# Unused identity products on TensorE while the first chunk's attention is computed

## Chip, core, metric

The kernel runs on one core of a Trainium2 chip. The metric is the device time of one execution in microseconds (us), median of several executions. Engines are named as the profile names them: PE is TensorE (PEld its weight loads), DVE is VectorE, ACT is ScalarE, POOL is GpSimd, SP is SyncE, whose queue here issues every DMA.

## What is computed

An attention block feeds two feed-forward blocks, all in float32. Cut to what matters:

```python
# q, k, v: (4, 8, 576, 64)
q_d, k_d, v_d = means of q, k, v over groups of 4 positions
out_up   = repeat(softmax(q_d k_d^T / 8) v_d, 4)
out_loc  = softmax(where(|i - j| < 4, q k^T / 8, -1e9)) v
x        = (out_up + out_loc) as (2304, 512)
h        = x @ w_in                      # 512 x 2048
x        = (h - tanh(h)) @ w_out         # 2048 x 512
gate     = sigmoid(x @ w_gate)           # 512 x 1536
out      = (gate * (x @ w_val)) @ w_out2 # 1536 x 512
```

## The kernel before

The 2304 tokens are cut into six chunks of 384. For each chunk the first feed-forward block runs over sixteen slices f of its hidden width: `do_h` makes a slice of h, `h_out` and `g_out` turn it into h - tanh(h), `do_y` multiplies that back and adds into four PSUM banks `acc0` to `acc3`. Each float32 product of these blocks is taken as three products of split operands (`mm3`, lines 227 to 229; the split is lines 221 to 223 and line 237).

Attention is emitted as a list of items. A "down" item (`down`) is the pooled attention of one pair of heads: scores (line 300), the maximum (line 315), exponentials (line 321), normalising (lines 282 to 288), two transposes by the identity `id_sb` (line 329) and the values (line 341). A "local" item (`local`) is the banded attention of six blocks of 64 queries: scores (line 367), scale and mask (lines 404 or 411), maximum (line 415), exponentials (line 419), normalising, transposes (line 427), values (line 435) and the addition of the two attentions (line 450). The pooled means of q and k are line 268 on DVE for the first batch, lines 270 to 272 on POOL for the others.

Nothing of the first feed-forward block can start before the attention of the first chunk, so the program begins with a loop (lines 626 to 634) that emits one attention item after the other and, between them, parts of the first two slices of h (`early_h`, banks `acc2` and `acc3`), loads of weights (`w_load`) and the conversion of weights from float64 bits to float32 (lines 168, 174, 176, 191). `tick` advances a counter by which later steps of an item are emitted. A second loop (lines 635 to 637) emits what is left of `early_h`. From line 638 on the first chunk's slices follow one another, with later attention items between them.

PSUM has eight banks here: `acc0` to `acc3` and four of tag `ab`. Every step of attention takes its bank from `a_bank`. While `startup[0]` is true, two of each six go to `acc0` and `acc1`, which `do_y` doesn't need yet; the other four go round the four `ab` banks.

The order on PE, DVE and ACT in this opening part is not the order of the code: a scheduler places the instructions of these engines from their dependences and its own costs. POOL's order is as written, SP's from the first chunk on, ACT's, DVE's and POOL's from the second chunk on.

Of the kernel before, what the change touches and what calls it, by code (L numbers as in the profile page):

```python
# [52 lines left out]
def tile_kernel(ctx: ExitStack, tc: tile.TileContext, qk, vp, v, w1, w2, mask, ident, out):  # L53
    nc = tc.nc
# [22 lines left out]
    id_sb = const.tile([128, 128], F32, name="id_sb")  # L77
# [3 lines left out]
    startup, spare = [True], [0]  # L81

    def acc_bank(e):
        return ps.tile([128, 512], F32, tag=f"acc{e}", name="acc")

    def a_bank():

        spare[0] += 1
        if startup[0] and spare[0] % 6 in (2, 4):
            return acc_bank(spare[0] % 6 // 2 - 1)  # L90
        return ps.tile([128, 512], F32, tag="ab", bufs=4, name="ab")


# [13 lines left out]
    def run_chains(todo):  # L107
        while todo:
            for g in list(todo):
                if next(g, True):  # L110
                    todo.remove(g)

    def tick():
        now[0] += 1
        run_chains(chains.pop(now[0], []))
        todo = events.get(now[0], [])
        while todo:
            fn, args = todo.pop(0)
            fn(*args)
        events.pop(now[0], None)  # L120
        if beat[0]:
            beat[0]()
# [6 lines left out]
    def raw_pool(i):  # L129
        if i < n_a:  # L130
            return rawp if i % (n_b + 1) == n_b else raw1
        if i < U1:
            return rawp
        return rawp if (i - U1) % 2 else wpools["raw2"]
# [12 lines left out]
    def w_load(limit):  # L147

        while loaded[0] < min(limit, n_units if "raw2" in wpools else U1):
            i = loaded[0]  # L150
            raws[i] = raw_pool(i).tile([128, WU], I64, tag="raw", name="raw")
            nc.sync.dma_start(out=raws[i], in_=w1[i] if i < U1 else w2[i - U1])
            load_at[i] = now[0]
            loaded[0] += 1
# [5 lines left out]
    def w_begin(limit=n_units):  # L160
        i = begun[0]
        if i >= min(limit, loaded[0]) or now[0] < load_at[i] + 5:
            return
        begun[0] += 1
        hi = words(i)[1].bitcast(F32)


        nc.scalar.activation(out=hi, in_=hi, func=ACTF.Prelu, scale=2.0 ** -112, alpha=2.0 ** 32)
        chain(2, w_bits, i)
        defer(5, w_high, i)  # L170
# [38 lines left out]
    def weight(l, f, j):  # L209

        i, at = (f, 512 * j) if l == 1 else divmod((3 * f + j) * 512, WU)
        i += U1 * (l - 1)
        while i not in wt:
            tick()
        return wt[i][:, :, at:at + 512]

    def have(l, f, j):
        return f in wt
# [74 lines left out]
    def down(u):  # L293
        m = means.pop(u)
        qd, kd = m[:, 0, :], m[:, 1, :]
        sd = a_bank()[:, :3 * SD].rearrange("p (j k) -> p j k", j=3)
        for j in range(3):
            for h in range(2):
# [27 lines left out]
        def turn(f):  # L326
            tb = a_bank()[:72, :384]
            for j in range(3):
                nc.tensor.transpose(  # L329
                    out=tb[:, 128 * j:128 * j + 128], in_=pd[:, j, 72 * f:72 * f + 72], identity=id_sb  # L330
                )

            kept = bass.AP(tensor=tb.tensor, offset=tb.offset, ap=[list(tb.ap[0]), [64, 2], [136, 3], [1, 48]])
            defer(1, copy, pdt[:, f], kept)

        def values():
            vd = vds.pop(u)
            ob = a_bank()[:, :SD]
            for h in range(2):
                for f in range(2):  # L340
                    nc.tensor.matmul(
                        out=ob[64 * h:64 * h + 64, :], lhsT=vd[:, f, 64 * h:64 * h + 64],
                        rhs=pdt[:, f, h].rearrange("p j k -> p (j k)"), start=(f == 0), stop=(f == 1),
                    )
            defer(1, copy, od[:, p % 2, :], ob)
# [153 lines left out]
    def item():  # L499

        fetch()
        x = items[started[0]]
        if x[0] == "d" and x[1] not in means:
            return 0
        started[0] += 1
        if x[0] == "d":
            down(x[1])
            return 4
        local(*x[1:])
        return 6  # L510
# [15 lines left out]
    def h_part(w, key, bank, k):  # L526
        wh, wl = (w[:, i, k * 128:(k + 1) * 128] for i in range(2))
        x = xt[key, k]
        mm3(bank[:, :N], wh, wl, x[:, 0, :], x[:, 1, :], k == 0, k == KD - 1)
# [11 lines left out]
    def h_out(c, f, hb):  # L541
        h_done.add((c, f))
        t = ts[c, f] = xs.tile([128, N], F32, tag="xs", name="t")
        nc.scalar.activation(out=t, in_=hb[:, :N], func=ACTF.Tanh)  # L544
        chain(1, subtract, t, hb[:, :N], t)
        defer(2, g_out, c, f)
# [66 lines left out]
    def early_h(n):  # L613
        for _ in range(n):
            if not early:
                return
            k, f = early[0]
            if ((1, 0), k) not in xt or not have(1, f, 0) or now[0] < seen.setdefault((k, f), now[0] + 3):
                return
            early.pop(0)  # L620
            h_part(weight(1, f, 0), (1, 0), hbs[f], k)
            if k == KD - 1:
                h_out(0, f, hbs[f])

    free = [0]
    while any(((1, 0), k) not in xt for k in range(KD)):
        if now[0] >= free[0] and started[0] < len(items):
            item()
        early_h(2)
        tick()  # L630
        w_load(min(loaded[0] + 1, 3))
        if started[0] % 3 == 0:
            w_begin(U1)
        tick()
    while early:
        early_h(1)
        tick()
    startup[0] = False

# [162 lines left out]
```

## Time and profile before

| | us |
|---|---|
| median of 3 runs (lowest, highest) | 1038.02 (1035.78, 1040.18) |
| the profiled execution | 1036.53 |
| its span, first to last instruction | 1034.7 |
| PE busy in the span | 992.7 (96%) |
| DVE busy | 422.3 (41%) |
| ACT busy | 373.1 (36%) |

The profiled execution's own time is 1.8 us longer than its span and 1.5 us shorter than the median. [...] Averages over the span hide the opening part, which is 85 us of 1035; it has to be read in windows.

### The profile page before, as it was taken

The numbers are of one execution on the slowest core, as the hardware profiler recorded it, in microseconds if no ns is written. First come the engines' busy times: TensorE is split into PE (matmuls) and PEld (weight loads), VectorE is DVE, ScalarE is ACT, GpSimd is POOL, SyncE is SP. The second block draws the span as 40 slices with busy tenths as digits, with TensorE's granted clock in tenths as the row PEclk, the third lists the DMA queues.
The fourth block names the chain that finished last, engine by engine and source line by source line (L and its number), as shares of the span: only waits on it lengthen the run. The fifth ranks groups of instructions, "written<-read, shape, count | busy, mean of one in ns | idle before, by whom it ended". The sixth has DMA issues, their size and how long they took to land.

```text
span 1034.7 us, 15463 instructions
## 1 busy us (share of the span) xinstructions
PE 992.7 (96%) x6392; PEld 923.6 (89%) x6392; DVE 422.3 (41%) x736; ACT 373.1 (36%) x951; POOL 81.5 (8%) x89
## 2 busy tenths in 40 slices
PE   3889999999999999999999999999999999999997
PEld 2658988999999899999999899999999999999996
DVE  5788774324334444433765654113211113211112
ACT  5666554334334344433643543113111113111111
POOL 2251220110110302000000000000000000000000
PEclk9568999999999999999999999999999999999998
DMA  9543732301301411203535231001100002000001
GB/s 295 182 167 114 259 87 78 93 24 56 107 3 55 125 28 47 78 17 120 167 111 185 89 123 41 1 23 39 61 1 1 1 24 69 32 1 1 1 1 62
DMA packets 33111, 76.74 MB, mean 74 GB/s; under 512 B 3264, under 2 KB 23184, under 8 KB 28688
## 3 DMA queue, kind: packets, MB, share of 16 engines
q1 hardware_dynamic: 33040, 75.75, 22.6%
q8 instruction: 50, 0.82, 0.3%
q14 instruction: 21, 0.17, 0.1%
HBM read 63.15 MB, written 12.58 MB: 73 GB/s over the span
## 4 chain that ended last, share of the span: by engine, by line
PE 88%; DVE 5%; ACT 3%; DMA 3%; issue 1%; POOL 0%; SPq 0%; DVEq 0%; ACTq 0%; POOLq 0%
PE ab L227 18%; PE ab L228 17%; PE ab L229 17%; PE acc L227 9%; PE acc L228 9%; PE acc L229 9%; PE ab L367 2%; PE ab L435 2%; PE ab L427 1%; PE ab L300 1%; DMA raw<-in_w 1%; DVE raw L176 1%; DMA qk<-in_qk 1%; DVE w L191 1%; PE ab L329 1%
## 5 line engine op out<-in xcount | busy, mean ns | idle before, releaser
L227 PE MATMUL ab<-x,w 128*128 128x384 f32 x952 | 326.7, 343 | 3.7 <-ACT x L237 3.7
L228 PE MATMUL ab<-x,w 128*128 128x384 f32 x952 | 322.4, 339 | 0.0
L229 PE MATMUL ab<-x,w 128*128 128x384 f32 x952 | 321.7, 338 | 0.0
L227 PEld LDWEIGHTS ab<-x,w 128*128 128x128 f32 x952 | 179.1, 188 | 10.6 <-ACT x L237 4.4
L228 PEld LDWEIGHTS ab<-x,w 128*128 128x128 f32 x952 | 179.4, 188 | 3.5 <-DVE x L222 0.3
L229 PEld LDWEIGHTS ab<-x,w 128*128 128x128 f32 x952 | 179.4, 188 | 0.0
L728 DVE TENSOR_TENSOR p<-ab,p 128x384 f32<-128x384 f32 x72 | 40.1, 557 | 277.6 <-PE ab L229 277.6
L227 PE MATMUL acc<-g,w 128*128 128x384 f32 x384 | 133.9, 349 | 0.0
L228 PE MATMUL acc<-g,w 128*128 128x384 f32 x384 | 129.9, 338 | 0.0
L229 PE MATMUL acc<-g,w 128*128 128x384 f32 x384 | 129.7, 338 | 0.0
L240 DVE TENSOR_TENSOR t<-ab,t 128x384 f32<-128x384 f32 x94 | 52.3, 556 | 156.8 <-ACT t L544 156.7
L724 ACT ACTIVATE p<-ab 128x384 f32<-128x384 f32 x72 | 35.3, 491 | 187.2 <-PE ab L229 187.2
L544 ACT ACTIVATE t<-ab 128x384 f32<-128x384 f32 x94 | 45.8, 487 | 153.3 <-PE ab L229 137.4
L237 ACT ACTIVATE g<-p 128x384 fp32r<-128x384 f32 x72 | 37.8, 525 | 157.5 <-DVE p L728 157.5
L227 PEld LDWEIGHTS acc<-g,w 128*128 128x128 f32 x384 | 72.1, 188 | 2.5 <-issue 2.0
L228 PEld LDWEIGHTS acc<-g,w 128*128 128x128 f32 x384 | 72.2, 188 | 0.1
L229 PEld LDWEIGHTS acc<-g,w 128*128 128x128 f32 x384 | 72.1, 188 | 0.0
L240 DVE TENSOR_TENSOR g<-t,g 128x384 fp32r<-128x384 f32 x96 | 56.1, 584 | 38.4 <-ACT g L237 37.6
L237 ACT ACTIVATE g<-t 128x384 fp32r<-128x384 f32 x96 | 50.2, 524 | 46.7 <-DVE t L240 46.7
L222 DVE TENSOR_TENSOR g<-p,g 128x384 fp32r<-128x384 f32 x72 | 40.2, 559 | 42.6 <-ACT g L237 42.6
L227 PE MATMUL acc<-w,g 128*128 128x512 f32 x144 | 57.0, 396 | 0.0
L229 PE MATMUL acc<-w,g 128*128 128x512 f32 x144 | 56.9, 395 | 0.0
(99 smaller groups left out, 1103.7 us busy)
## 6 DMA issues: line engine op xcount, KB each, us to landing
raw<-in_w SPq DMA_DIRECT2D x34, 1024.0 KB
qk<-in_qk SPq DMA_DIRECT2D x16, 576.0 KB
vr<-in_vp SPq DMA_DIRECT2D x16, 288.0 KB
out<-o SPq DMA_DIRECT2D x18, 256.0 KB
x<-xo SPq DMA_DIRECT2D x20, 192.0 KB
xs<-x SPq DMA_DIRECT2D x20, 192.0 KB
y<-y SPq DMA_DIRECT2D x20, 192.0 KB
xs<-y SPq DMA_DIRECT2D x20, 192.0 KB
```

The lines of the kernel that those rows point to most:

```text
L176: nc.vector.scalar_tensor_tensor(out=lo, in0=hi, scalar=3, in1=lo, op0=ALU.logical_shift_left, op1=ALU.bitwise_or)
L222: nc.vector.tensor_tensor(out=dst[:, 1, :], in0=src, in1=dst[:, 0, :].bitcast(F32), op=ALU.subtract)
L227: nc.tensor.matmul(out=o, lhsT=wh, rhs=xh, start=first, stop=False)
L228: nc.tensor.matmul(out=o, lhsT=wh, rhs=xl, start=False, stop=False)
L229: nc.tensor.matmul(out=o, lhsT=wl, rhs=xh, start=False, stop=last)
L237: nc.scalar.activation(out=dst, in_=src, func=ACTF.Copy)
L240: nc.vector.tensor_tensor(out=dst, in0=a, in1=b, op=ALU.subtract)
L367: nc.tensor.matmul(out=sb[r0:r0 + 64, x, :], lhsT=t[r0:r0 + 64, 0, QB * j:QB * j + QB], rhs=t[r0:r0 + 64, 1, w0:w0 + WIN], start=True, sto ...
L435: nc.tensor.matmul(out=ob[r0:r0 + 64, QB * x:QB * x + QB], lhsT=vw[0][:, j - n, i, r0:r0 + 64], rhs=pt[:, x, r0:r0 + 64], start=True, stop ...
L544: nc.scalar.activation(out=t, in_=hb[:, :N], func=ACTF.Tanh)
L724: nc.scalar.activation(out=p, in_=gate[:, :N], func=ACTF.Sigmoid)
L728: nc.vector.tensor_tensor(out=p, in0=val[:, :N], in1=p, op=ALU.mult)
```

## The change

`a_bank` no longer hands out `acc0` in the opening part: one of each five banks is `acc1`, the other four go round the `ab` banks. `acc0` is instead allocated once as `idle`. A new function `keep_warm(n)` emits n products of the identity with itself (128 x 128 by 128 x 128, float32) into it; nothing reads them. It is called with 2 at two places of the loop of the opening part and at one place of the loop behind it, 110 products in all.

```diff
     def a_bank():
 
         spare[0] += 1
-        if startup[0] and spare[0] % 6 in (2, 4):
-            return acc_bank(spare[0] % 6 // 2 - 1)
+        if startup[0] and spare[0] % 5 == 2:
+            return acc_bank(1)
         return ps.tile([128, 512], F32, tag="ab", bufs=4, name="ab")
...
+    def keep_warm(n):
+
+        for _ in range(n):
+            nc.tensor.matmul(out=idle[:, :128], lhsT=id_sb, rhs=id_sb, start=True, stop=True)
+
+    idle = acc_bank(0)
     free = [0]
     while any(((1, 0), k) not in xt for k in range(KD)):
+        keep_warm(2)
         if now[0] >= free[0] and started[0] < len(items):
             item()
         early_h(2)
         tick()
+        keep_warm(2)
         w_load(min(loaded[0] + 1, 3))
         if started[0] % 3 == 0:
             w_begin(U1)
         tick()
     while early:
         early_h(1)
+        keep_warm(2)
         tick()
     startup[0] = False
```

The scheduler doesn't leave the products where they are written. Line 628 is the product; lines behind 622 are numbered 9 higher in the changed kernel.

PE at the start of the program, from the first pooled scores to the second ones. Before:

```order
L300 MATMUL ab<-m 64x144 x6
L329 MATMUL ab<-id_sb,pd 72x128 x3
L329 MATMUL acc<-id_sb,pd 72x128 x3
L367 MATMUL ab<-qk 64x70 x12
L341 MATMUL ab<-pdt,vd 64x144 x4
L367 MATMUL ab<-qk 64x70 x12
L300 MATMUL acc<-m 64x144 x6
```

The same place now:

```order
L300 MATMUL ab<-m 64x144 x3
L628 MATMUL acc<-id_sb 128x128 x2
L300 MATMUL ab<-m 64x144 x3
L628 MATMUL acc<-id_sb 128x128 x15
L329 MATMUL ab<-id_sb,pd 72x128 x6
L628 MATMUL acc<-id_sb 128x128
L367 MATMUL ab<-qk 64x70 x12
L628 MATMUL acc<-id_sb 128x128 x2
L341 MATMUL ab<-pdt,vd 64x144
L300 MATMUL acc<-m 64x144 x6
```

Seventeen products stand ahead of the first transposes of `pd`, and the second local scores (the other row L367) have moved behind the second pooled scores.

PE from the third pooled scores to the first products of the feed-forward block (x is the split attention, w the weights). Before:

```order
L300 MATMUL ab<-m 64x144 x6
L341 MATMUL ab<-pdt,vd 64x144 x4
L427 MATMUL ab<-id_sb,pl 70x128 x8
L435 MATMUL acc<-pt,vw 64x64 x6
L427 MATMUL ab<-id_sb,pl 70x128
L427 MATMUL acc<-id_sb,pl 70x128 x3
```

The same place now:

```order
L628 MATMUL acc<-id_sb 128x128 x14
L300 MATMUL ab<-m 64x144 x6
L427 MATMUL ab<-id_sb,pl 70x128 x6
L427 MATMUL acc<-id_sb,pl 70x128 x3
L427 MATMUL ab<-id_sb,pl 70x128 x3
L435 MATMUL ab<-pt,vw 64x64 x12
L628 MATMUL acc<-id_sb 128x128 x18
L427 MATMUL acc<-id_sb,pl 70x128 x3
L628 MATMUL acc<-id_sb 128x128
L227 MATMUL acc<-x,w 128x384 x2
```

Two clumps, of 14 and of 18, stand ahead of work that others wait for. There are 23 such places; the other clump of 14 stands between the transposes (line 427) of the third pair of heads and those of the fourth.

DVE at the first local scores (pl is the masked scores, nb the maxima). Before:

```order
L268 TENSOR_REDUCE m<-qk 128x288
L411 SCALAR_TENSOR_TENSOR pl<-ab,mask_sb 128x420 x2
L315 TENSOR_REDUCE nb<-acc 128x3
L415 TENSOR_REDUCE nb<-pl 128x6
L317 TENSOR_SCALAR nb<-nb 128x3
```

The same place now:

```order
L411 SCALAR_TENSOR_TENSOR pl<-ab,mask_sb 128x420
L191 TENSOR_TENSOR w<-raw,w 128x1024
L315 TENSOR_REDUCE nb<-acc 128x3
L415 TENSOR_REDUCE nb<-pl 128x6
L317 TENSOR_SCALAR nb<-nb 128x3
L174 TENSOR_SCALAR raw<-raw 128x1024
L176 SCALAR_TENSOR_TENSOR raw<-raw 128x1024
L282 TENSOR_SCALAR ss<-ss 128x3
L286 RECIPROCAL ss<-ss 128x3
L288 TENSOR_TENSOR pd<-pd,ss 128x432
L174 TENSOR_SCALAR raw<-raw 128x1024
L411 SCALAR_TENSOR_TENSOR pl<-acc,mask_sb 128x420
```

The mask of the second pair's local scores has moved behind the second pooled softmax, since its scores are now in `acc1`, the bank that the second pooled scores occupied; weight conversion (lines 174, 176, 191) has moved ahead of it.

## Rows read from the trace of the kernel before

**Rows 1.** The page: shares of the span, PE and granted clock in 40 slices.
```profile
PE 992.7 (96%) x6392; PEld 923.6 (89%) x6392; DVE 422.3 (41%) x736; ACT 373.1 (36%) x951; POOL 81.5 (8%) x89
...
PE   3889999999999999999999999999999999999997
...
PEclk9568999999999999999999999999999999999998
```
**Rows 2.** Busy us by stretch (start:end, length; PE, PEld, DVE, ACT, POOL; clock).
```profile
0.00:85.00 85.00, 58.23 (x528) 43.68 (x528) 62.22 (x103) 51.91 (x174) 32.51 (x35) 0.70 0.65 214
85.00:157.00 72.00, 69.52 (x527) 64.38 (x528) 53.50 (x81) 43.04 (x104) 14.19 (x12) 1.00 0.45 145
```
**Rows 3.** The same view, cut where the clock rose or fell.
```profile
22.10:32.20 10.10, 4.62 (x30) 3.20 (x29) 9.43 (x12) 7.23 (x18) 4.48 (x4) 0.50 0.70 217
32.40:35.60 3.20, 1.80 (x30) 1.17 (x28) 2.95 (x7) 3.00 (x11) 1.94 (x3) 1.00 0.63 266
35.80:52.60 16.80, 15.53 (x158) 12.58 (x157) 11.35 (x23) 11.98 (x38) 2.65 (x3) 0.50 0.54 167
52.80:59.50 6.70, 4.22 (x36) 3.27 (x36) 6.67 (x12) 4.46 (x19) 6.46 (x6) 1.00 0.32 111
59.70:83.40 23.70, 21.51 (x157) 15.44 (x159) 17.93 (x27) 13.66 (x50) 10.81 (x11) 0.50 0.57 189
```
**Rows 4.** Timeline of PE, start and us: the same work at both clocks.
```profile
36.48 1.70 PE L300 MATMUL ab<-m 64*64 64x144 f32 x12 [0.68 <-DVE m L268]
...
45.65 1.67 PE L367 MATMUL ab<-qk 64*64 64x70 f32 x24
...
53.86 0.82 PE L329 MATMUL ab<-id_sb,pd 128*72 128x128 f32 x6
...
54.78 0.95 PE L300 MATMUL ab<-m 64*64 64x144 f32 x12
...
79.69 1.50 PE L329 MATMUL ab<-id_sb,pd 128*72 128x128 f32 x6
...
87.95 0.95 PE L367 MATMUL ab<-qk 64*64 64x70 f32 x24
```
**Rows 5.** Chain that ended last, start and us: ends of two stretches on PE.
```profile
39.56 0.71 PE acc L341 x2
...
49.75 1.62 PE ab L367 x24
...
69.11 0.74 PE acc L341 x2
...
82.78 0.32 PE acc L227
83.11 0.88 PE ab L341 x8
```
**Rows 6.** Waits of DVE for PE, 0 to 85 us, first and last of seven.
```profile
DVE pl L411 <- PE ab L367: 3.5, 3, 1.3
...
DVE pl L404 <- PE ab L427: 0.2, 1, 0.2
```
**Rows 7.** Waits of PE, 0 to 85 us: total, times, longest.
```profile
PE ab L300 <- DVE m L268: 12.7, 3, 6.6
...
PE ab L329 <- ACT raw L168: 3.3, 1, 3.3
```
**Rows 8.** Timeline of DVE: first and second local scores masked; one weight converted.
```profile
14.71 0.60 DVE L411 SCALAR_TENSOR_TENSOR pl<-ab,mask_sb 128x420 f32<-128x420 f32 x1
...
16.52 0.60 DVE L411 SCALAR_TENSOR_TENSOR pl<-ab,mask_sb 128x420 f32<-128x420 f32 x1 [1.22 <-PE ab L367]
...
115.51 1.23 DVE L191 TENSOR_TENSOR w<-raw,w 128x1024 fp32r<-128x1024 f32 x1 [0.20 <-ACT w L237]
```
**Rows 9.** Timeline of ACT and PE: exponentials of the second pooled scores; that weight's use.
```profile
19.46 0.37 ACT L321 ACTIVATE pd<-acc,nb 128x144 f32<-128x144 f32 x1
...
127.96 0.42 PE L227 MATMUL ab<-x,w 128*128 128x384 f32 x1
```

## The prediction

> **What bounds the kernel now.** Read the page first: PE is busy for 96% of the span, and the slices show where it is not at its best, the first three, in which the granted clock stands at 9, 5 and 6 tenths and then 8 before it stays at 9 [rows 1]. The averages of the rest say little, so the second view is the windows. In the first 85 us PE is busy for 58.23, DVE for 62.22 and ACT for 51.91 of 85; from 85 to 157, while the first chunk goes through the feed-forward block, PE is busy for 69.52 of 72 at full clock [rows 2]. From 85 us on the kernel is PE at full clock, so what the change can win or lose lies in the first 85 us, and a microsecond there reaches the end as long as the stage behind keeps up.
>
> The third view is the same windows cut at the clock's steps [rows 3]. PE runs at half clock in three stretches, with 4.62, 15.53 and 21.51 us of matmuls in them, 41.7 together. (The first 22 us are shown at 1.00, but the first pooled scores there last as long as those at half clock, so some of them are slow too.) Two things are to be seen. The clock fell at 35.7 and at 59.6 behind stretches in which PE worked 1.80 of 3.20 and 4.22 of 6.70 us. And it did not rise for 16.8 us in which PE worked 15.53: these were for the most part small products of attention and transposes.
>
> The fourth is the timeline, for what a full clock is worth: twelve records of pooled scores take 1.70 us at half and 0.95 at full clock, 24 of local scores 1.67 and 0.95, six transposes 1.50 and 0.82 [rows 4]. That is a ratio of 0.56, not 0.5. The fifth, the chain of waits, says that half clock is on the path: it runs on PE from 39.56 to 51.37 without leaving it, and again from 69.11 to 83.99 [rows 5].
>
> **The change: what a full clock could give.** The 41.7 us at half clock would take 41.7 x 0.56 = 23.4, so 18.3 us of PE time go. Of the chain's two long stretches (11.8 and 14.9 us) 26.7 x 0.44 = 11.7 us would go. Late next is DVE: it has 62.2 us of its own in the 85, none of which shrinks, and it waits for the first load and for ACT besides. What it can get back is its waits for PE, which are seven rows from 3.5 down to 0.2 us, 11.3 in all [rows 6]. Chain and DVE give the same ceiling, 11.3 to 11.7; I take 11.3.
>
> **What the products cost.** The trace has no full 128 by 128 float32 product of 128 columns. Nearest are the transposes, 128 columns against a weight of 72: 0.82 / 6 = 0.14 us at full clock, 1.50 / 6 = 0.25 at half [rows 4]. Plain float32 products are recorded as two passes (12 products of line 367 are 24 records), transposes as one, so a product is two of these: 0.27 at full and 0.50 at half clock. The bounds are one pass, 0.14, and two at half clock, 0.50. I take 0.25, since two passes of one weight follow each other closely. 110 of them are 27.5 us at full, 55 at half clock.
>
> They lie beside PE's waits. PE has 85 - 58.2 = 26.8 us without work, 6.6 of them before the first data, and its longest waits are for the means on DVE (12.7 us in three, the 6.6 among them) and for the first softmax (3.3) [rows 7]. With 18.3 us given back by the clock there is room for 27.5 us: 39.9 + 27.5 = 67.4, against 85 - 11.3 - 6.6 = 67.1 if the whole ceiling were reached. So PE would then be full to the brim, in an order fixed beforehand, and the ceiling isn't reached. What is lost I price at the clumps. The first, 15 products, takes 3.8 us at full clock and stands where PE waited 3.3; it starts at half clock and ends some 2 us late, which the other 6.1 us of waits for means behind it swallow. The first clump of 14 takes 3.5 and stands where PE had 10.10 - 4.62 = 5.5 us free: nothing. The clump of 18 takes 4.5 where PE had 1.4 free [rows 3]: 3.1 late. The second clump of 14 takes 3.5 where 2.5 were free: 1.0 late, about what the small ones that find no gap cost. Waiting behind them on PE are transposes and values of local attention, and for these ACT, then DVE's addition and split of x. I put the loss at 3.3.
>
> **Banks and order.** One bank less means that a step waits sooner for the reader of the bank's last content. The place where it shows is the second local scores: they were masked at 16.52 [rows 8]; now they wait for the exponentials of the second pooled scores, which end at 19.8 [rows 9], so they are 4 to 6 us later. ACT and DVE have the weight conversion to do meanwhile, which has moved ahead, and ACT ran the exponentials of both local scores back to back; so I cost it at nothing, and at 4 where that cover is gone. The DMA queue's order changes only by places of one or two; nothing there.
>
> **Behind 85 us.** The stage needs weights and attention of the next chunk. The weight whose conversion starts at 115.51 [rows 8] is first used at 127.96 [rows 9], 11.2 us after it is done, and its DMA is released by work that moves ahead with PE. DVE is at 53.50 of 72 [rows 2]. So the gain is carried through, less perhaps 1 us, which is inside the range.
>
> **The sum.** 11.3 - 3.3 = 8.0 us. The profiled execution's 1036.5 becomes 1028.5; it lies 1.5 under the median of 1038.0, and I forecast the median: 1030.0.
>
> [...]
>
> **Rivals.** First, the products fill gaps, but the clock does not follow, since what keeps it low is the small work itself. Then only the stretch with the real gap is cured (22.1 to 32.2, 4.62 us of work: 2.0 us), and the others stay as they are: 1036. For it: the 15.53 of 16.80 us at half clock. Against it: the products use all of the array, and the clock did rise behind 83.4 [rows 3], right after products of 128 x 128 with 384 columns, the last of them at 82.78 [rows 5]. That is also the case in which the change doesn't do what it says. [...]
>
> Second, DVE and ACT keep their time: the waits of DVE for PE turn into waits for ACT, and the later second local scores cost their 4 us: 8 - 4 = 4 us, 1034. For it: DVE is busy 9.43 of 10.10 and 6.67 of 6.70 us in two of the stretches [rows 3].
>
> Third, and on the other side: the clumps run at half clock. A clump of 18 is then 9.0 us where 1.4 were free, the second of 14 is 7.0 where 2.5 were free, 12.1 us late together on the path of x; the clock gives back only the quarter of the path (3 to 4 us) that lies right behind the clumps: 8 us slower, 1046. It decides once the overshoot of the clumps (12.1 at half, 4.1 at full clock) is more than what the clock returns, which is about when it is up for less than half of the opening part. For it: the clock fell twice in stretches with over half of the time busy. Against it: a clump is the densest work that the opening part has.
>
> **How the numbers follow.** The forecast and what lies around it (gain over 5.2 us) 0.55; all of the ceiling or more, by an order that also helps DVE (over 12 us, under 1026) 0.06; the first and second rival together 0.23; the third 0.16. A difference under 0.5%, 5.2 us, can hardly be told from none in this kernel. So faster 0.61, same 0.23, slower 0.16. The forecast alone spans 1025 to 1033 (product at 0.14 to 0.35 us, loss of 0 to 6); with the first two rivals and the near part of the third the range is 1022 to 1043, which leaves out about 0.04 below and 0.12 above.
>
> **What would show it.** Right: the clock at 1.00 through most of the first 80 us; the product at about 0.25 us; the split of x complete some 8 us earlier; PE dense from about 77 instead of 85; DVE's waits for PE mostly gone and DVE busier than 75% there; from there to the end the same length. Wrong: clock rows at 0.50 over 20 us or more; the product near 0.5 us; new waits of ACT or DVE for PE right behind clumps; or a longer stage between 85 and 157.

## The result and the profile after

| | before | after |
|---|---|---|
| median (lowest, highest), us | 1037.53 (1035.78, 1040.18) | 1023.32 (1023.05, 1025.82) |
| the profiled execution | 1036.53 | 1023.21 |
| its span | 1034.7 | 1021.4 |
| mean granted clock in the span | 0.971 | 0.998 |

The granted clock is PE's, as the profile gives it: a share, 1.00 at its highest in these traces and 0.50 in the stretches called half clock. The ratio is 0.9866, with a 95% interval of 0.984 to 0.9893: the change saves 14.2 us by the medians and 13.3 by the spans. The sign was forecast, and the mechanism. The size was not: the sum gave 8.0 us. What came lies in the case that had a chance of 0.06, a gain of over 12 us.

The page of after, the shares and the slices that answer to [rows 1]:

```profile
PE 998.4 (98%) x6612; PEld 936.2 (92%) x6612; DVE 421.5 (41%) x736; ACT 372.3 (36%) x951; POOL 81.0 (8%) x89
...
PE   7999999999999999999999999999999999999996
...
PEclk9999999999999999999999999999999999999999
```

PE has 220 records more, two for each of the 110 products, and only 5.7 us more busy time, since the same real work went at a faster clock (0.998 in the mean, not 0.971). The windows of after, as in [rows 2] (length; busy us of PE, PEld, DVE, ACT, POOL; granted clock, DMA share, GB/s):

```profile
0.00:85.00 85.00, 75.41 (x842) 66.77 (x843) 69.52 (x118) 59.35 (x196) 32.64 (x35) 1.00 0.73 231
85.00:157.00 72.00, 69.69 (x527) 64.46 (x526) 50.05 (x75) 39.33 (x92) 13.41 (x12) 1.00 0.42 138
```

The granted clock of the first 85 us went from 0.70 to 1.00, and DVE did 7.3 us more of its work there. Where the gain appears along the program can be read from four landmarks in the timelines of the two kernels:

| landmark | before | after | gain so far |
|---|---|---|---|
| fourth split of the first chunk's x begins (DVE, line 222) | 76.47 | 67.89 | 8.6 |
| first product of the third slice (PE, line 227) | 85.68 | 76.92 | 8.8 |
| end of a wait of PE for `pl`, near the end of the first chunk | 156.98 | 146.60 | 10.4 |
| transfer `xs<-y` ahead of the second feed-forward block (line 520) | 563.62 | 552.98 | 10.6 |
| end of the span | 1034.7 | 1021.4 | 13.3 |

So 8.8 us come from the opening part, 1.6 from the rest of the first chunk, 0.2 from there to the second block, and 2.7 from beyond that.

**What the products did in the opening part.** Timeline of PE of after (start, us, operation; the number behind x counts records, two for a product):

```profile
7.85 1.22 PE L628 MATMUL acc<-id_sb 128*128 128x128 f32 x4
9.00 1.22 PE L300 MATMUL ab<-m 64*64 64x144 f32 x6
10.15 5.60 PE L628 MATMUL acc<-id_sb 128*128 128x128 f32 x30
15.59 0.82 PE L329 MATMUL ab<-id_sb,pd 128*72 128x128 f32 x6
...
16.56 0.95 PE L367 MATMUL ab<-qk 64*64 64x70 f32 x24
...
33.60 4.29 PE L628 MATMUL acc<-id_sb 128*128 128x128 f32 x36
37.78 0.52 PE L427 MATMUL acc<-id_sb,pl 128*70 128x128 f32 x3
...
54.35 3.29 PE L628 MATMUL acc<-id_sb 128*128 128x128 f32 x28
57.53 0.49 PE L427 MATMUL ab<-id_sb,pl 128*70 128x128 f32 x3
```

The first six records of pooled scores and the first two products are slow (1.22 us for 6 records, against 0.95 for 12 later), although the clock is shown at 1.00 there too. The work speeds up within the clump of 15 products: its first 18 records take 4.00 us (10.15 to 14.15), its last 12 take 1.44 (14.15 to 15.59). Behind it six transposes take 0.82 us and 24 records of local scores 0.95: the durations of full clock in [rows 4]. They keep them to the end of this part: the local scores at 65.76 take 0.95, six transposes at 73.44 take 0.82.

Some rows of the chain of after (start, us, what; its lengths are those between steps, so a little shorter than the timeline's):

```profile
7.92 1.15 PE acc L628 x4
9.07 1.15 PE ab L300 x6
10.22 5.53 PE acc L628 x30
...
27.00 3.32 PE acc L628 x28
30.32 0.94 PE ab L300 x12
...
36.74 0.59 DVE pl L288
```

Two products in 1.15 us are 0.575 each, ahead of the point at which the work speeds up; in the first 18 records of the clump it is 0.44 a product, and 14 in 3.32 are 0.237 at full clock. And from 6.7 to 33.7 us the chain is on PE without a break, products included: there they are the path, no filling. Behind that it is mostly on DVE until x is complete.

### The profile page after: what moved, and what is told of

The parts are those of the page before. It is cut to its first block, busy times and chain, and to the rows that moved or that the text cites. A ratio compares the mean times of both kernels' runs of the same rounds, so it can differ in the third digit from the quotient of the medians.

```text
span 1021.4 us, 15900 instructions
## 1 busy us (share of the span) xinstructions
PE 998.4 (98%) x6612; PEld 936.2 (92%) x6612; DVE 421.5 (41%) x736; ACT 372.3 (36%) x951; POOL 81.0 (8%) x89
## 4 chain that ended last, share of the span: by engine, by line
PE 88%; DVE 6%; DMA 3%; ACT 2%; issue 1%; POOL 0%; SPq 0%; DVEq 0%; ACTq 0%; POOLq 0%
PE ab L227 18%; PE ab L228 17%; PE ab L229 17%; PE acc L227 9%; PE acc L228 9%; PE acc L229 9%; PE ab L367 2%; PE acc L628 2%; PE ab L435 2%; DMA raw<-in_w 1%; PE ab L427 1%; DVE raw L176 1%; PE ab L300 1%; DVE w L191 1%; DMA qk<-in_qk 1%
```

## Experiments

All edits are given against the changed kernel. "Clock" is the mean granted clock from 20 to 100 us, "x" the start of the fourth split of x, "slice 3" the first product of the third slice, "block 2" the start of the first transfer `xs<-y`; each of these is from the run's one profile.

| kernel | unused work | clock | x | slice 3 | block 2 | median us |
|---|---|---|---|---|---|---|
| before | none | 0.68 | 76.47 | 85.68 | 563.62 | 1037.53 |
| after | 110 products | 1.00 | 67.89 | 76.92 | 552.98 | 1023.32 |
| e1_banks | none | 0.77 | 72.42 | 80.29 | 561.11 | 1035.46 |
| e2_corner | 110 of 32 rows and columns | 0.81 | 90.44 | 102.12 | 580.56 | 1048.70 |
| e3_turns | 220 transposes | 1.00 | 63.26 | 74.80 | 550.39 | 1021.62 |
| e4_half | 55 products | 0.87 | 74.10 | 81.45 | 559.92 | 1030.06 |
| e5_early | 48 products | 0.87 | 70.62 | 75.60 | 553.52 | 1024.11 |
| e6_late | 62 products | 0.81 | 68.86 | 76.94 | 559.24 | 1031.58 |
| e7_six | 108 products, six banks | 0.94 | 71.96 | 82.69 | 561.82 | 1032.55 |
| e8_double | 220 products | 1.00 | 77.74 | 99.90 | 575.19 | 1046.79 |
| e9_nolast | 76 products | 0.94 | 66.86 | 72.19 | 550.84 | 1023.83 |
| e10_turns_nolast | 152 transposes | 0.98 | 64.24 | 69.33 | 549.75 | 1019.60 |
| e11_turns_lean | 124 transposes | 0.94 | 69.87 | 75.16 | 555.25 | 1026.39 |
| e12_five_acc3 | 108 products, five banks | 1.00 | 67.77 | 77.89 | 553.69 | 1024.81 |

**The change without its products.** The five-bank rotation stays, all three calls go:

```diff
-        keep_warm(2)
```

> The bank rotation of the change alone: one of five banks is acc1, acc0 is allocated and unused, and no product is emitted. Theory (the gain comes from TensorE's clock in the opening part): the clock stays at 0.50 in three stretches as before, and the time is that of before, 1037 us, or up to 4 us longer by the later second local scores: 1034 to 1042, ratio 0.997 to 1.004. Rival (the gain comes from the other order of DVE, ACT and the banks): much of the 14 us is here already, 1024 to 1030.

Measured: 1035.46 us, ratio 0.9978 (0.9966 to 0.999). Windows of e1_banks, cut to the three places where the clock was low:

```profile
24.00:43.00 19.00, 12.48 (x78) 8.44 (x77) 15.84 (x29) 13.41 (x43) 5.33 (x6) 0.50 0.55 192
61.00:70.00 9.00, 6.86 (x61) 5.54 (x62) 5.18 (x12) 4.85 (x10) 3.31 (x4) 0.50 0.63 218
81.00:88.00 7.00, 7.00 (x61) 6.31 (x60) 5.51 (x8) 1.65 (x3) 2.90 (x3) 0.51 0.41 115
```

Banks and the order that goes with them are worth 2.6 us against the kernel before in the same batch of runs (1038.1). In the opening part they are worth more, 5.4 us at the third slice, but there the clock is down again, 0.51 from 81 to 88 while PE is busy throughout, and at the second block 2.5 are left.

**The same order, smaller products.** The scheduler places these products exactly as the changed kernel's on every engine, so only what a product does differs:

```diff
-            nc.tensor.matmul(out=idle[:, :128], lhsT=id_sb, rhs=id_sb, start=True, stop=True)
+            nc.tensor.matmul(out=idle[:32, :128], lhsT=id_sb[:32, :32], rhs=id_sb[:32, :], start=True, stop=True)
```

> All instructions, banks and orders of the change, but each product uses a corner of the array: 32 rows and 32 columns of the identity as the weight, 128 columns streamed as before. Theory (the products raise the clock because they are full work of the array): the clock falls again, the first scores up to 85 us are at 0.50 in long stretches, and since the products then cost about 0.5 us each instead of 0.23, the time is that of before or longer: 1033 to 1048. Rival A (any unbroken stream on TensorE holds the clock): clock at 1.00 from 10 us on and the time of the change, 1022 to 1026. Rival B (the order is what gains): 1022 to 1028 with the clock at 0.50.

Measured: 1048.70 us, ratio 1.01 (1.0075 to 1.0125), slower than before. Window of e2_corner, then its timeline of PE:

```profile
20.00:100.00 80.00, 76.94 (x701) 57.86 (x697) 56.53 (x96) 48.06 (x164) 24.68 (x24) 0.81 0.48 152
```

```profile
10.21 6.60 PE L628 MATMUL acc<-id_sb 32*32 32x128 f32 x30
16.74 1.49 PE L329 MATMUL ab<-id_sb,pd 128*72 128x128 f32 x6
...
31.75 1.67 PE L367 MATMUL acc<-qk 64*64 64x70 f32 x24
...
36.46 4.00 PE L628 MATMUL acc<-id_sb 32*32 32x128 f32 x28
```

PE is busy for 76.94 of these 80 us, as in the changed kernel (77.10), and yet the clock is 0.81 instead of 1.00. Even that is too high, since the clock is shown at 1.00 up to about 35 us: behind the first clump the transposes take 1.49 us, not 0.82, and at 31.75 the local scores are still at 1.67. From there to the fourth split of x the clock is 0.72:

```profile
35.40:90.40 55.00, 53.13 (x503) 40.59 (x502) 38.17 (x68) 35.64 (x120) 14.76 (x15) 0.72 0.45 149
```

A mean of 0.72 over 55 us is some 31 us at half clock; together with the first 35 us, of which the changed kernel has some 14 (its work sped up within the first clump, at 14.15), that is about 52 us more. By the 0.56 of [rows 4] they should cost 52 x 0.44, some 23 us (an estimate); the split of x is 22.6 us later. A corner product is no dearer by itself: two take 0.62 us at full clock (56.44), as against 0.61 in the changed kernel (74.09). So work of the same count in the same order ends 25.4 us apart, and the clock is the difference. The time is near the prediction's third rival (1046), but the picture is not quite its own: only the clumps of the first 35 us run at half clock, the later large ones (28 records in 4.00 us from 36.46, 0.29 a product, at a clock of 0.85 from 36 to 40) mostly at full, and it is real work between them that is slow.

**How many.** Half and twice the count:

```diff
-        keep_warm(2)
+        keep_warm(1)
```

> One product at each of the three places instead of two, 55 in all; they now stand in eight clumps. Theory (the products in the first 30 us stand on the path and cost, while the clock needs only some of them): if the clock holds, 1 to 3 us faster than the change, 1020 to 1023; where it falls for a stretch of 10 us of work, 4 us are lost again: 1024 to 1030. Rival (a product costs nothing because it only fills gaps): no faster than the change, 1023 to 1030.

```diff
-        keep_warm(2)
+        keep_warm(4)
```

> Four products at each place, 220 in all, 51 us of TensorE at 0.23 us each. Theory: the clock is at 1.00, and what is more than the idle time (about 10 us are left in the changed kernel's first 77 us) lies on the path: 25 us more work, 10 to 18 us slower than the change, 1033 to 1041. Rival (they only fill gaps, the scheduler sees to it): 1023 to 1026.

Measured: 55 products 1030.06 us, ratio 0.9916 (0.9897 to 0.9935); 220 products 1046.79, ratio 1.0087 (1.0066 to 1.0107). Windows of e4_half, then of e8_double:

```profile
39.00:50.00 11.00, 10.13 (x108) 7.93 (x106) 7.67 (x14) 5.74 (x14) 0.00 (x0) 0.56 0.69 233
64.00:74.00 10.00, 9.63 (x90) 7.24 (x91) 6.27 (x12) 5.68 (x15) 1.94 (x3) 0.57 0.71 228
```

```profile
60.00:101.00 41.00, 38.55 (x411) 36.44 (x410) 21.53 (x36) 19.33 (x61) 10.03 (x11) 1.00 0.34 110
```

With 55 the clock still falls twice. With 220 it never does, but DVE works for 21.53 of 41 us: PE has become the bound, with products between all of its real work, one clump of 16 as late as 95.00, and the loss is larger than the 10 to 18 us expected. Full clock by itself is no gain then. From none to 220 the medians are 1035.5, 1030.1, 1023.3 and 1046.8. The count was not changed alone, though: the scheduler put all of the 55 ahead of 33.3 us, while those of the changed kernel go on to 77.

**Transposes in place of products.**

```diff
-        for _ in range(n):
-            nc.tensor.matmul(out=idle[:, :128], lhsT=id_sb, rhs=id_sb, start=True, stop=True)
+        for _ in range(2 * n):
+            nc.tensor.transpose(out=idle[:, :128], in_=id_sb, identity=id_sb)
```

> Two transposes of the identity in place of each product (220, the same time on TensorE by the transposes of before: 0.14 us each at full clock). Theory as by the trace of before (long stretches of small products and transposes stayed at 0.50): the clock stays low for much of the opening part, the transposes cost 0.25 us each, 55 us against 26.8 us without work: slower than before, 1040 to 1060. [...] Rival (a busy TensorE is enough): as with the products, 1022 to 1028.

Measured: 1021.62 us, ratio 0.9843 (0.9827 to 0.986). Timeline of PE of e3_turns:

```profile
9.91 4.57 PE L628 MATMUL acc<-id_sb 128*128 128x128 f32 x28
14.32 0.82 PE L329 MATMUL ab<-id_sb,pd 128*72 128x128 f32 x6
...
70.73 1.09 PE L628 MATMUL acc<-id_sb 128*128 128x128 f32 x8
...
72.18 1.91 PE L628 MATMUL acc<-id_sb 128*128 128x128 f32 x16
```

The clock stands at 1.00 from 20 to 100 us. The expectation that transposes would not bring it up fell; they do as well as products. The rows at 70.73 and 72.18 show the second thing: x is split at 63.26, 4.6 us sooner than in the changed kernel, but then transposes stand between the products of line 227 to 229, and the third slice begins only 2.1 us sooner.

**By the place in the code.** Only while the attention items of the first half are begun, and only after:

```diff
-        for _ in range(n):
+        for _ in range(n if now[0] < 24 else 0):
```

> Products only while the emission counter is under 24: the first 48 of the 110, which stood before 30 us in the changed kernel. Theory (clock in the opening part; each stretch that falls back costs its own share): full clock to about 33 us, then 0.50 in long stretches as in the run with the bank rotation alone; the products are on the path there, so little or nothing is gained against that run (1035.5): 1032 to 1038. Rival (the gain is made in the first 30 us): 1023 to 1028.

```diff
-        for _ in range(n):
+        for _ in range(n if now[0] >= 24 else 0):
```

> Products only from counter 24 on: the other 62. Theory: the opening runs as in the run with the bank rotation alone up to some 35 us, without 11 us of products on TensorE's path there, and at full clock afterwards: as fast as the change or up to 4 us faster, 1019 to 1025. Rival (the early products are needed, because a full clock early moves all that follows): 1027 to 1033.

Measured: the early 48 products 1024.11 us, ratio 0.9873 (0.9858 to 0.9887); the late 62 1031.58, ratio 0.9926 (0.9897 to 0.9955), with one of its four executions at 1025.43. Both expectations fell. But the second edit did not do what it was meant to: "late" holds for the code alone. The first and the last products in the timeline of PE of e6_late:

```profile
8.34 3.53 PE L628 MATMUL acc<-id_sb 128*128 128x128 f32 x22
...
31.31 1.95 PE L628 MATMUL acc<-id_sb 128*128 128x128 f32 x16
```

The scheduler put all 62 between 8.3 and 33.3 us; the 48 of e5_early end at 28.9, the 55 of e4_half at 33.3. So these three runs have all of their products in the same stretch, and no run shows what products in the second half alone are worth. What they do show is that more products are not better by themselves (48, 55 and 62: 1024.1, 1030.1 and 1031.6 us), and that the clock first falls some us behind the last of them, at 36 to 38 us. Windows of e5_early, then of e6_late:

```profile
52.00:70.00 18.00, 14.44 (x132) 11.03 (x134) 11.96 (x23) 10.81 (x37) 9.40 (x11) 0.53 0.47 160
```

```profile
75.00:87.00 12.00, 11.17 (x80) 10.34 (x81) 8.40 (x13) 4.67 (x8) 1.91 (x3) 0.58 0.56 193
```

e5_early comes within 0.8 us of the changed kernel, although its clock is down for some 18 us. e6_late is down from 37 to 44 and from 55 to 68 as well, and still level with the changed kernel at the third slice (76.94); then it loses 6.2 us by the second block, most of it where the clock is 0.58 from 75 to 87. That fits a half clock which costs little where DVE is the path and much where PE is, but the orders of the two kernels differ too, and nothing takes that apart.

**Without the last ones.** The call in the second loop goes, with products and with transposes; and transposes with fewer of them behind the first half:

```diff
     while early:
         early_h(1)
-        keep_warm(2)
         tick()
```

> The change without the products of the second loop (the one behind the last attention item of the opening): the first 76 of 110, the order up to about 50 us is that of the change. Theory (clock in the first 50 us carries the gain; later products cost on TensorE what they return): 1022 to 1025, with the clock falling once behind 52 us as in the run with the early products alone (1024.1). Rival (the later products hold a clock that is worth several us): 1026 to 1030.

> The same with two transposes for each product (152 of 220). In the run with all 220, some 3.5 us of transposes stood behind 70 us between the last products of the first two slices, with the split of x long complete. Theory: without them the dense part starts up to 3 us earlier, but the clock may fall once behind 55 us, which costs 2 to 3 us: 1018 to 1023. Rival (the late ones are needed): 1024 to 1030.

```diff
-        for _ in range(n):
+        for _ in range(2 * n if now[0] < 24 else n):
```

> Two transposes for each product while the emission counter is under 24, one after that, none in the second loop: 124. Theory: less work in front of the same clock, 1018 to 1024; where the clock falls earlier than with 152, up to 1028.

Measured: 76 products 1023.83 us, ratio 0.9873 (0.9854 to 0.9891); 152 transposes 1019.60, ratio 0.9824 (0.9808 to 0.984); 124 transposes 1026.39, ratio 0.9893 (0.9877 to 0.9908). The window of the opening part of e10_turns_nolast:

```profile
0.00:85.00 85.00, 73.08 (x802) 62.65 (x803) 70.82 (x120) 59.93 (x198) 33.52 (x35) 0.98 0.72 231
```

With transposes the last calls cost what e3_turns showed: without them the third slice begins at 69.33 instead of 74.80. In part that is because other work now stands behind it (574 records of PE from there to the first split of the next chunk's x, 550 in e3_turns); at that split 2.5 us are left (147.22 against 149.72), and 2.0 by the medians. It is the lowest median of all versions, 17.6 us under the kernel before in its batch (1037.24), 3.7 under the changed kernel's; its four executions (1018.51 to 1021.39) overlap with those of e3_turns (1020.74 to 1023.38), not with the changed kernel's. DVE does 70.82 us of its work in the window, more than in the changed kernel. With products the gain at the third slice (72.19 against 76.92) shrinks the same way: 576 records follow up to the next chunk's split, against 550, and there 1.7 us are left (150.47 against 152.18). Then the clock falls once more in the second block, as shown further down, and the median is that of the changed kernel. Fewer still, e11_turns_lean, whose transposes end at 35.4 us, gives 6.8 us back, with the clock down for 10 us from 57.7.

**The bank.** The products into the free columns of `acc3`, where they need no bank of their own, first with the six-bank rotation of before and then with five:

```diff
-        if startup[0] and spare[0] % 5 == 2:
-            return acc_bank(1)
+        if startup[0] and spare[0] % 6 in (2, 4):
+            return acc_bank(spare[0] % 6 // 2 - 1)
...
-        for _ in range(n):
-            nc.tensor.matmul(out=idle[:, :128], lhsT=id_sb, rhs=id_sb, start=True, stop=True)
-
-    idle = acc_bank(0)
+        shut = len(early) > 2 * KD - 2
+        for _ in range(n if early else 0):
+            nc.tensor.matmul(out=hbs[1][:, N:], lhsT=id_sb, rhs=id_sb, start=shut, stop=shut)
```

> The products of the change with the bank rotation of before: they go into the 128 columns that bank acc3 has free beside the second slice of h (a hardware accumulation is open there, so they add instead of starting anew; 108 products), and acc0 stays with attention. Theory: clock at 1.00; the rotation alone was worth 2.6 us, so without it the time is 1 to 4 us longer than the change: 1024 to 1028. Rival (a sixth bank takes waits away): 1019 to 1022.

> Five banks in rotation as in the change, products in the free columns of acc3 as in the run with six banks (1032.5): it parts the two things that run changed at once. If the sixth bank was what made that run slow: 1022 to 1026. If the place was (products tied to the slice of h that is added up in that bank, so that they are late and stand behind the waits of that slice): 1029 to 1034. I expect the place.

 (The second part of the diff alone.)

Measured: six banks 1032.55 us, ratio 0.9954 (0.9939 to 0.9968); five banks 1024.81, ratio 0.9878 (0.9863 to 0.9893). Waits of DVE in the first 85 us (total, times, longest), of e7_six and then of e12_five_acc3:

```profile
DVE nb L315 <- PE ab L300: 6.3, 3, 3.6
```

```profile
DVE nb L315 <- PE ab L300: 4.2, 2, 3.6
```

Both expectations fell: e7_six was expected at 1024 to 1028 or below, and e12_five_acc3 at 1029 to 1034. The place of the products is not what made e7_six slow: with five banks and the same place the time is that of the changed kernel within 1.5 us. Six banks cost 7.7 us here, and they cost 2.6 without any products (before against e1_banks). One more wait of the maximum for pooled scores fits the 4.2 us that the split of x is later (71.96 against 67.77). Another part is the clock, which e12_five_acc3 keeps at 1.00 and e7_six loses twice, the second time behind its last product, where PE is busy throughout:

```profile
82.00:88.00 6.00, 6.00 (x58) 4.99 (x56) 2.74 (x5) 2.75 (x6) 0.00 (x0) 0.50 0.30 78
```

Why more banks do worse is not settled: the scheduler writes another order for each rotation, and the number of banks was not tried in one and the same order.

## Why the prediction was right, and where its sum was off

**The clock.** Right. Full clock through the opening part was the mechanism, the first rival (the clock does not follow) is out by the 1.00 in the windows, and e2_corner shows that the gain hangs on it. But not every microsecond of it counts: e5_early has all but 0.8 us of the gain with the clock at 0.53 from 52 to 70.

**The price of a product.** 0.25 at full and 0.50 at half clock were worked out from transposes; the rows show 0.237 at full clock, and ahead of it 0.575 for the first two and 0.44 within the clump. Right at full clock, between the two at half. The step from 0.27 down to 0.25 was an estimate; the 28 records of a clump stand 0.119 us apart on average (3.32 us).

**The sum in the opening part.** 8.0 us were forecast at the third slice and 8.8 came, so up to there the net is right, but not term by term, and that it is so near is in part luck. It was also forecast as the clock's alone, with banks and order at nothing: e1_banks, without any products, has 5.4 of the 8.8 us at the third slice and, once the clock has fallen again behind it, 2.6 of the 14.2 at the end.

**The ceiling, 11.3 us.** Mis-sized, since it counted only DVE's waits for PE, the 11.3 us of [rows 6]. On the way to the fourth split of x, DVE's time divides like this, its waits summed from the rows of its view of waits, its work from the window up to there:

| DVE until the split of x is due | before, 76.5 us | after, 67.9 us | less |
|---|---|---|---|
| waits for the first load | 5.2 | 5.3 | -0.1 |
| waits for PE | 10.1 | 6.5 | 3.6 |
| waits for ACT | 4.1 | 1.4 | 2.7 |
| own work | 56.25 | 53.92 | 2.3 |
| not in the rows | 0.9 | 0.8 | 0.1 |

The windows that give the own work, of before and of after:

```profile
0.00:76.50 76.50, 50.23 (x470) 37.35 (x470) 56.25 (x94) 46.95 (x154) 28.43 (x32) 0.71 0.67 218
```

```profile
0.00:67.90 67.90, 58.69 (x693) 51.30 (x695) 53.92 (x93) 45.17 (x154) 25.48 (x29) 1.00 0.74 233
```

Only a third of the waits for PE came back, not most of them. The largest left is the wait for the first pooled scores, which grew:

```profile
DVE nb L315 <- PE ab L300: 3.6, 1, 3.6
```

Before, it was 1.81 us. Two products now stand in the middle of these scores, at 0.575 us each. What came back beside it had been held fixed. The waits for ACT are 2.7 us shorter, which fits scores that reach ACT sooner, though no run takes this apart. And the own work is 2.3 us less, mostly in two lines (operation, pieces; busy us, mean ns; idle before), first of before, then of after:

```profile
L174 DVE TENSOR_SCALAR raw<-raw 128x1024 int32<-128x1024 int32 x8 | 5.9, 740 | 0.0
...
L282 DVE TENSOR_SCALAR ss<-ss 128x3 f32<-128x3 f32 (+1 forms) x12 | 4.2, 347 | 3.0 <-ACT pd L321 2.4 <-ACT pl L419 0.6
```

```profile
L174 DVE TENSOR_SCALAR raw<-raw 128x1024 int32<-128x1024 int32 x7 | 4.8, 684 | 0.0
...
L282 DVE TENSOR_SCALAR ss<-ss 128x3 f32<-128x3 f32 (+1 forms) x12 | 2.6, 219 | 0.8 <-ACT pd L321 0.7
```

One piece of weight conversion went behind the split, and of the twelve short operations of line 282, which mostly take 0.16 us, four took 0.65 to 0.82 before and one 0.68 after. What goes with a long one the traces show. Timeline of POOL and DVE of before:

```profile
53.27 1.70 POOL L276 TENSOR_TENSOR vd<-vr 72x256 f32<-72x256 f32 x1
...
54.31 0.69 DVE L282 TENSOR_SCALAR ss<-ss 128x6 f32<-128x6 f32 x1
```

The short operation ends at 55.00, 0.03 us behind the operation of POOL beside it. So do all five long ones, and those without an operation of POOL beside them take 0.16 to 0.17 us. So at these five places DVE's own work was longer, by 0.5 to 0.7 us each, where it met POOL, and another order changes where that is. "Banks and order" were costed at nothing, and e1_banks, with 50.67 us of own work and no products, shows that they have a part in this. The second mask is 8.4 us later (16.52 to 24.95), more than the 4 to 6 forecast; that costs nothing which shows, as forecast, since e1_banks, where it is at 22.86, is faster than before.

**The loss, 3.3 us.** About the right order of size, in the wrong places. The clump of 18 was to be 3.1 late: the `pl` for which the work behind it waited was written at 37.33 and that work began at 37.78, so it cost 0.4. The second clump of 14 was to cost 1.0 and cost nothing, since its `pl` was ready at 57.38, its successor at 57.53. The clumps priced at nothing, early, did cost: transposes at 15.59 instead of 11.60, 4.0 late and not 2; third pooled scores at 30.31 instead of 28.04; fourth mean at 37.26 instead of 35.02. The prediction had seen room for the first clumps in PE's waits, and didn't see that with 17 products ahead PE works without a break until 33.7 us. This was won back later at the faster clock.

**Behind 85 us, less perhaps 1.** Wrong in sign, and here lies most of what the forecast missed: 1.6 us more by the end of the first chunk, 0.2 to the second block, 2.7 between the two blocks. The 1.6 are mostly work that PE has already done. From the third slice to the wait at the end of the chunk it is busy for 68.92 of 71.30 us before:

```profile
85.70:157.00 71.30, 68.92 (x524) 63.75 (x522) 52.80 (x80) 42.34 (x103) 14.19 (x12) 1.00 0.46 146
```

and for 67.64 of 69.70 after:

```profile
76.90:146.60 69.70, 67.64 (x500) 63.10 (x498) 52.25 (x78) 41.14 (x100) 14.96 (x13) 1.00 0.45 151
```

Among its groups, 24 records of local values (0.9 us) and three transposes (0.5) stand in this stretch before and ahead of it after. And 2.7 more arise between the two blocks, at a place that the change doesn't touch. Timeline of PE of before, then of after, at the first product of the second block:

```profile
570.38 0.62 PE L227 MATMUL ab<-x,w 128*128 128x384 f32 x2 [3.15 <-ACT x L237]
```

```profile
558.56 0.62 PE L227 MATMUL ab<-x,w 128*128 128x384 f32 x2 [1.96 <-ACT x L237]
```

Before, the first transfer `xs<-y` took 6.17 us and PE waited 3.15, and the clock fell behind that wait:

```profile
571.00:575.00 4.00, 4.00 (x14) 4.00 (x15) 3.90 (x9) 3.98 (x8) 0.00 (x0) 0.57 0.00 0
```

After, it took 4.98, PE waited 1.96, and the clock stayed at 1.00. A short wait is no safeguard, though. The same place in e9_nolast, timeline of PE and then the window behind it:

```profile
556.46 0.61 PE L227 MATMUL ab<-x,w 128*128 128x384 f32 x2 [2.01 <-ACT x L237]
```

```profile
558.10:561.40 3.30, 3.30 (x12) 3.30 (x11) 3.19 (x7) 3.28 (x6) 0.00 (x0) 0.50 0.00 0
```

From this transfer to the next one of its kind the profiles fall into three groups. Before, e1_banks, e6_late and e11_turns_lean take 113.7 to 113.8 us: PE waits 3.15 to 3.19 and the clock falls. e4_half, e9_nolast and e10_turns_nolast take 112.5 to 112.8: PE waits 1.98 to 2.17 and the clock falls all the same. The other seven take 111.0 to 111.3: PE waits 1.91 to 2.25 and the clock stays. So of the 2.7 us some 1.2 are the longer wait and 1.5 the half clock behind it. Kernels that do not differ there fall into each group, and the falls at least change from execution to execution: those of e10_turns_nolast list mean clocks of 0.993, 0.994, 0.997 and 0.997 and took 1021.39, 1020.25, 1018.94 and 1018.51 us. The first is the profiled one, whose clock falls near 57, 334 and 556 us, and a mean of 0.997 has no room for all three, of some 3.4 us each. The medians, 14.2 us apart over four executions each, speak against luck in two profiles alone. What the traces tie to the change is 10.6 us.

**The rivals.** The second (DVE and ACT keep their time) is half true: behind 33.7 us the chain is mostly on DVE, and that is what bounds the gain now. The third did not come here: e2_corner, with its first clumps and much of its real work at half clock, ends near the time that it gives, and e8_double is slower by another way, full clock with too much to do.

## To carry to other kernels

Here a stage full of small products had a mean granted clock of 0.70, and with 110 unused products of 128 by 128 among them it had 1.00. Where the same is tried elsewhere, look in the trace for where the unused work ended up and where the clock still falls: here a scheduler put 48, 55 and 62 products all into the first 33 us, and they gave 1024.1, 1030.1 and 1031.6 us. 220 were so many that they became the bound, and the last 34 of the 110, where real work is dense, brought nothing (e9_nolast). Cost the gain on the engine that waits, with all of its waits and the order of its own work, not only its waits for TensorE; and build the side effects (here a bank less) alone, since a scheduler can move the time with them. Half clock seems to have cost most where TensorE itself was the path (0.8 us lost to the changed kernel in e5_early, at 0.53 from 52 to 70; 6.2 in e6_late between the third slice and the second block, most of it at 0.58 from 75 to 87), so read the clock behind the stage too.

## What the runs showed of the hardware

- Unused transposes by the identity held the granted clock at 1.00 from 20 to 100 us just as products did (e3_turns, 1021.62 us), and 152 of them gave the lowest median (1019.60).
- Products on 32 rows and 32 columns did not (e2_corner): PE busy for 76.94 of 80 us at a mean clock of at most 0.81, against 77.10 at 1.00 with 128 by 128. Whether the rows or the columns count was not tried.
- The clock shown was no guide early in the program: in the changed kernel it reads 1.00 from the start, while the first products take 0.575 us and later ones 0.237; in the kernel before it reads 1.00 at 6.58 us, where twelve records of pooled scores take 1.71 us, as long as at 0.50 (1.70).
- In the middle of products of 128 by 128 with 384 columns, at the second block, four waits of 3.15 to 3.19 us were each followed by some 3.4 us at half clock. Of ten waits of 1.91 to 2.25 us three were (1.98, 2.01 and 2.17), so the length of the wait alone does not decide.
- A DVE operation on 128 by 3 or 128 by 6 that takes 0.16 us took 0.65 to 0.82 at five places, four of before and one of after, up to the fourth split of x; each time it ended 0.03 us behind an operation of POOL that had begun before it.
